# A chunked linear-attention stage in front of a dense layer: chunks of 64 steps of two batches on 64x64 tiles of the matrix array

## The chip, the cores and the metric

The kernel runs on one core of a Trainium2 chip. The core has a matrix engine (TensorE: PE for its matmuls, PEld for its weight loads), a vector engine (DVE), a scalar engine (ACT), GpSimd (POOL) and SyncE (SP), which here only issues DMAs. TensorE reads SBUF and writes the eight PSUM banks; DVE and ACT read PSUM, POOL does not. The metric is the device time of one launch in microseconds (us); lower is better.

## The reference

Four batches, eight heads, 768 steps, head size 48. For each batch and head, with a decay w and a bonus u per channel:

```python
for t in range(S):
    y[t] = r[t] @ (state + outer(u * k[t], v[t]))
    state = w[:, None] * state + outer(k[t], v[t])
```

The outputs are laid side by side over the heads (3072 tokens by 384), and a dense block follows: `h = x @ w_in` (384 by 2048), `g = h - tanh(h)`, `out = g @ w_out` (2048 by 384). The weights arrive as 64-bit floats, so the kernel rebuilds 32-bit ones from their bits.

## The kernel before

**Units and blocks.** The attention is cut into 24 units of one batch and one chunk of 128 steps (`C`). Two units make a block of 256 tokens, held transposed in a tile `xt`, and the dense layer runs block by block. `drive` (L177) sets the order: blocks 0 and 1 of the attention are woven with the 28 steps that load and convert the weights; then `dense(j)` is woven with the attention of block j+2, for j from 0 to 9; `dense(10)` and `dense(11)` have no attention beside them. The framework orders each engine's instructions by priority and by its own estimate of readiness and puts the semaphores in; an engine then works through its list in order.

**One unit** (`unit`, L310) has six steps, between which the weave may put dense work. The heads lie in four pairs, each padded to two times 64 rows or columns.

- POOL scales k and r by powers of the decay (`kw` L317, `rw` L318), PE transposes both (four 128x128 transposes each, L323), ACT copies them to SBUF as `kT` and `rT` (L325). POOL multiplies r, k and u (L330, L331).
- DVE sums that product to the bonus `du` (L334), POOL forms `dv` = v times `du` (L336), PE forms the scores `lev` = k against r, eight matmuls on 48 rows, which lie in the upper or the lower half of the array (L342).
- DVE copies the strictly earlier half of the scores to `at` by a mask (two instructions, L345).
- PE forms `y_p`: four matmuls with the running state (L350, not in a batch's first chunk) and eight with `at` and v (L354); DVE adds `dv` (L357).
- PE forms the state's increment `kv_p` (L362, not in a batch's last chunk), DVE adds it to the state (two instructions, L369), POOL multiplies by the chunk's decay (L373). PE transposes y (three transposes, L376) and ACT copies it to `xt` (L377).

**Dense** (`make_dense`, L118): for each pair of 128-column slices of `w_in`, six matmuls of 256 columns give `h` (L129); ACT, DVE and POOL form `g` in ten instructions (L140 to L149), of which DVE has five; two pairs later, four matmuls of 384 columns add to `o` (L155). ACT copies `o` out (L169), SP stores it (L171).

**Records.** All data are 32-bit floats, and the profile shows every matmul that is not a transpose as two weight loads and two matmuls: eight matmuls of `lev` are x16 in a row.

**Queues and tables.** r, k and v are loaded two units ahead by three DMAs on SP's queue (`fetch`, L300). Weights come by one DMA per tile on ACT's queue (L90) into two staging tiles, and are converted by one ACT, five DVE and two POOL instructions (L97 to L104). Ahead of all units, DVE makes the tables of the powers of the decay (L252 to L259), which PE turns (L265). A second version of the attention (`anywhere`, L384) runs only when a decay lies outside W_LOW to W_HIGH; with these inputs it does not.

Of the kernel before, what the change touches and what calls it, by code (L numbers as in the profile page):

```python
# [27 lines left out]
W_LOW, W_HIGH = 0.7, 1.4  # L28

C = 128  # L30
PAD = 64
AHEAD = 2
L = 2
# [13 lines left out]
class Dims:  # L47
    def __init__(self, r, moe_w_in):
        self.B, self.H, self.S, self.D = r.shape
        self.DM, self.DFF = moe_w_in.shape  # L50
        self.NP = self.H // 2
        self.NCH = self.S // C
        self.NU = self.NCH * self.B
        self.NK = self.DM // 128
        self.NF = self.DFF // 128
# [19 lines left out]

def weight_steps(nc, stage, w_in_sb, w_out_sb, moe_w_in, moe_w_out, d):
    V, A, G = nc.vector, nc.scalar, nc.gpsimd
    w_in_v = moe_w_in.rearrange("(ko ki) f -> ki ko f", ki=128)
    w_out_v = moe_w_out.rearrange("(ko ki) f -> ki ko f", ki=128)

    def weight(dst, src, cols):
        if src.dtype == F32:
            return lambda: nc.scalar.dma_start(out=dst, in_=src)


        assert src.dtype == I64
# [22 lines left out]
    for q in range(d.DFF // 512):  # L109
        for ko in range(d.NK):  # L110
            sl = slice(q * 512, (q + 1) * 512)
            weights.append(weight(w_in_sb[:, ko, sl], w_in_v[:, ko, sl], 512))
        for f in range(4 * q, 4 * q + 4):
            weights.append(weight(w_out_sb[:, f, :], w_out_v[:, f, :], d.DM))
# [3 lines left out]
def make_dense(nc, work, gpool, ps_d, w_in_sb, w_out_sb, m1b, m2b, out, d):  # L118
# [3 lines left out]
    def dense(j, xt):  # L122
# [43 lines left out]
        for i in range(L):  # L166
            c, b = divmod(L * j + i, d.B)
# [36 lines left out]
def near(ctx, tc, r, k, v, w, u, out, shared, weights):  # L204
# [42 lines left out]
    by = fixed("by", [128, NP, C + 1])  # L247
    plus = fixed("plus", [128, NP, C + 1])
    power = fixed("power", [128, NP, C + 1])
    inverse = fixed("inverse", [128, NP, C + 1])  # L250
    V.memset(by[:, :, 0:1], 0.0)
    V.tensor_copy(by[:, :, 1:], wcol[:, :, None].to_broadcast([128, NP, C]))  # L252
# [5 lines left out]
    wn = fixed("wn", [128, NP])  # L258
    V.tensor_copy(wn[:, :, None], power[:, :, C : C + 1])  # L259

    def turned(name, src, at):

        ps = ps_a.tile([128, 512], F32, name="tab_p", tag="tp")
        for p in range(NP):
            T.transpose(ps[:, p * 128 : (p + 1) * 128], src[:, p, at : at + C], ident)  # L265
        t = fixed(name, [128, H, D])
        A.copy(t, ps.rearrange("s (h d) -> s h d", h=H)[:, :, :D])
        return t

    w_up = turned("w_up", power, 0)  # L270
    w_down = turned("w_down", inverse, 1)

# [6 lines left out]
    before = fixed("before", [128, C])  # L279
    G.memset(before, 1.0)  # L280
    G.affine_select(out=before, in_=before, compare_op=ALU.is_ge, fill=0.0, base=-1,
                    pattern=[[1, C]], channel_multiplier=-1)
    before = before.bitcast(I32)

    def zeroed(name, count, shape):
        tiles = [fixed(f"{name}{i}", shape) for i in range(count)]
        for t in tiles:
            G.memset(t, 0.0)
        return tiles

    kws = zeroed("kw", 2, [128, H, PAD])
    rws = zeroed("rw", 2, [128, H, PAD])
    ats = [zeroed(f"at{i}_", 2, [128, NP, C]) for i in range(2)]
    states = zeroed("state", B, [128, NP, 2, D])

    dense = make_dense(nc, work, gpool, ps_d, shared["w_in"], shared["w_out"], shared["m1b"],
                       shared["m2b"], out, d)
    loaded = {}

    def fetch(n):  # L300
        c, b = divmod(n, B)
        rows = slice(c * C, (c + 1) * C)
        tiles = []
        for name, src in (("kt", k), ("rt", r), ("vt", v)):
            t = load.tile([128, H, D], F32, name=name, tag=name)
            nc.sync.dma_start(out=t, in_=src[b, :, rows, :].rearrange("h t d -> t h d"))
            tiles.append(t)
        loaded[n] = tiles

    def unit(n, xt, slot):  # L310

        c, b = divmod(n, B)
# [3 lines left out]
        state, kw, rw = states[b], kws[n % 2], rws[n % 2]  # L316
        G.tensor_tensor(kw[:, :, :D], kt, w_down, ALU.mult)  # L317
        G.tensor_tensor(rw[:, :, :D], rt, w_up, ALU.mult)  # L318
        turned = []
        for name, src in (("kT", kw), ("rT", rw)):  # L320
            ps = ps_a.tile([128, NP, C], F32, name="t_p", tag="tp")
            for p in range(NP):
                T.transpose(ps[:, p, :], src[:, 2 * p : 2 * p + 2, :].rearrange("t h d -> t (h d)"), ident)  # L323
            t = work.tile([128, NP, C], F32, name=name, tag=name)
            A.copy(t, ps)  # L325
            turned.append(t)
        kT, rT = turned

        rk = work.tile([128, H, D], F32, name="rk", tag="rk")
        G.tensor_tensor(rk, rt, kt, ALU.mult)  # L330
# [4 lines left out]
        dv = work.tile([128, H, D], F32, name="dv", tag="dv")  # L335
        G.tensor_tensor(dv, vt, du[:, :, None].to_broadcast([128, H, D]), ALU.mult)  # L336

        at = [ats[i][n % 2] for i in range(2)]
        lev = [ps_a.tile([128, NP, C], F32, name=f"lev{i}", tag=f"lev{i}") for i in range(2)]
        for p in range(NP):  # L340
            for i in range(2):
                T.matmul(lev[i][:, p], kT[HEAD[i], p, :], rT[HEAD[i], p, :], start=True, stop=True)  # L342
        yield
        for i in range(2):
            V.copy_predicated(at[i], before[:, None].to_broadcast([128, NP, C]), lev[i])  # L345
        yield
        y_p = ps_a.tile([128, NP, 2, D], F32, name="y_p", tag="ky")
        for p in range(NP):
            if c:
                T.matmul(y_p[:, p].rearrange("t i e -> t (i e)"), rT[:, p, :],  # L350
                         state[:, p].rearrange("d i e -> d (i e)"),
                         start=True, stop=False, skip_group_check=True)
            for i in range(2):
                T.matmul(y_p[:, p, i, :], at[i][:, p, :], vt[:, 2 * p + i, :],  # L354
                         start=c == 0, stop=True, skip_group_check=True)
        y = work.tile([128, H * D], F32, name="y", tag="y")
        V.tensor_tensor(y, y_p.rearrange("t p i e -> t (p i e)"), dv.rearrange("t h e -> t (h e)"), ALU.add)  # L357
        yield
        if c < d.NCH - 1:
            kv_p = ps_a.tile([128, NP, 2, D], F32, name="kv_p", tag="ky")  # L360
            for p in range(NP):
                T.matmul(kv_p[:, p].rearrange("d i e -> d (i e)"),  # L362
                         kw[:, 2 * p : 2 * p + 2, :].rearrange("s h d -> s (h d)"),
                         vt[:, 2 * p : 2 * p + 2, :].rearrange("s h e -> s (h e)"),
                         start=True, stop=True)
            for i in range(2):
                rows = HEAD[i]
                if c:
# [283 lines left out]
```

## Time and profile before

| | |
|---|---|
| median of 3 runs (lowest, highest) | 768.67 us (766.57, 769.08) |
| the profiled execution, its own time | 770.07 us |
| its span, first to last instruction | 768.3 us |
| mean granted TensorE clock | 0.961 of full speed |
| busy share of the span: PE, DVE, POOL, ACT | 88%, 69%, 49%, 38% |
| matmuls and weight loads recorded | 3280 and 3280 |

The span is cut into the time before about 200 us, in which the weights are converted, and the time after it. A matmul's recorded duration holds its way through the array, so that neighbours overlap; what one costs in a stream is the distance between starts. The chain of waits is followed back from the last instruction to what released each step.

### The profile page before, as it was taken

To read this page: it belongs to the slowest core of one execution; us is meant where nothing else is said; L and a number is where in the kernel's file an instruction comes from. 1 tells how busy PE (TensorE), PEld (TensorE's weight loads), DVE (VectorE), ACT (ScalarE), POOL (GpSimd) and SP (SyncE) were. 2 spreads that over 40 slices of the span, in tenths; PEclk is the share of its full clock that TensorE was granted. 3 is DMA by queue.
4 is the path that set the end of the run, shared out by engine and by line. 5 is a ranking of instruction groups with operands and counts; after the bars stand their busy time and mean duration, and the time that the engine had idled before them with its cause. 6 is when DMAs were issued, how large, how long until landed. Compare 5 with 4: busy or idle time off the path is not lost.

```text
span 768.3 us, 9268 instructions
## 1 busy us (share of the span) xinstructions
PE 678.2 (88%) x3280; PEld 513.8 (67%) x3280; DVE 532.9 (69%) x779; ACT 289.7 (38%) x511; POOL 379.9 (49%) x312
## 2 busy tenths in 40 slices
PE   1357769376999999999999999999999999999996
PEld 0246547254776876876776777778778777777774
DVE  9779999989675664864765765666646646566573
ACT  1114232214343533533534434334435345344432
POOL 6979966767344544534634543543534323223221
PEclk9999778767899999999999999999999999999999
DMA  7333343232011101102111111111100000000000
GB/s 185 87 105 106 93 113 83 80 79 68 22 31 37 37 12 47 25 11 52 22 27 36 32 22 31 32 21 32 22 20 21 1 22 0 1 21 0 22 1 26
DMA packets 82986, 32.35 MB, mean 42 GB/s; under 512 B 76146, under 2 KB 79347, under 8 KB 82931
## 3 DMA queue, kind: packets, MB, share of 16 engines
q1 hardware_dynamic: 78898, 19.08, 11.2%
q10 hardware_dynamic: 4032, 12.58, 5.4%
q8 instruction: 28, 0.46, 0.2%
q14 instruction: 28, 0.22, 0.1%
HBM read 26.94 MB, written 4.72 MB: 41 GB/s over the span
## 4 chain that ended last, share of the span: by engine, by line
PE 74%; DVE 12%; POOL 7%; issue 3%; DMA 2%; ACT 1%; ACTq 0%; DVEq 0%; POOLq 0%
PE h L129 31%; PE o L155 28%; PE y_p L354 5%; PE lev L342 3%; PE y_p L350 3%; PE t_p L323 2%; POOL part L103 2%; PE kv_p L362 2%; DVE cube L148 2%; DMA st<-in_moe_w_in_dram 2%; DVE cube L147 1%; DVE part L98 1%; DVE st L100 1%; DVE g L149 1%; POOL rk L330 1%
## 5 line engine op out<-in xcount | busy, mean ns | idle before, releaser
L129 PE MATMUL h<-xt,w_in_sb 128*128 128x256 f32 x1152 | 280.2, 390 | 11.9 <-POOL w_in_sb L104 11.6
L155 PE MATMUL o<-w_out_sb,g 128*128 128x384 f32 x768 | 272.4, 501 | 17.8 <-DVE g L149 17.8
L144 POOL TENSOR_SCALAR small<-s 128x512 f32<-128x512 f32 x96 | 147.9, 1541 | 213.7 <-ACT s L140 204.7
L129 PEld LDWEIGHTS h<-xt,w_in_sb 128*128 128x128 f32 x1152 | 215.9, 195 | 45.4 <-POOL w_in_sb L104 12.3
L155 PEld LDWEIGHTS o<-w_out_sb,g 128*128 128x128 f32 x768 | 147.9, 195 | 108.7 <-DVE g L149 12.9
L145 DVE SCALAR_TENSOR_TENSOR cube<-s,h 128x512 f32<-128x512 f32 x96 | 65.8, 685 | 176.6 <-ACT th L141 176.4
L140 ACT ACTIVATE s<-h 128x512 f32<-128x512 f32 x96 | 57.3, 597 | 191.7 <-issue 131.6
L149 DVE COPY_PREDICATED g<-small,cube 128x512 f32<-128x512 int32 x96 | 85.6, 892 | 5.2
L148 DVE SCALAR_TENSOR_TENSOR cube<-q,cube 128x512 f32<-128x512 f32 x96 | 80.0, 834 | 8.2
L147 DVE SCALAR_TENSOR_TENSOR cube<-q,cube 128x512 f32<-128x512 f32 x96 | 74.8, 779 | 0.0
L354 PE MATMUL y_p<-vt,at 128*128 128x48 f32 x384 | 58.9, 282 | 12.9 <-DVE at L345 12.9
L142 ACT ACTIVATE q<-s,m1b 128x512 f32<-128x512 f32 x96 | 69.3, 722 | 0.0
L143 ACT ACTIVATE q<-s,m2b 128x512 f32<-128x512 f32 x96 | 69.0, 718 | 0.6 <-DVE cube L148 0.6
L354 PEld LDWEIGHTS y_p<-vt,at 128*128 128x128 f32 x384 | 55.5, 208 | 17.7 <-DVE at L345 15.3
L146 DVE TENSOR_TENSOR g<-h,th 128x512 f32<-128x512 f32 x96 | 65.5, 682 | 0.0
L141 ACT ACTIVATE th<-h 128x512 f32<-128x512 f32 x96 | 56.8, 591 | 0.0
L336 POOL TENSOR_TENSOR dv<-vt,du 128x384 f32<-128x384 f32 x24 | 24.2, 1007 | 60.5 <-DVE y L357 60.5
L103 POOL TENSOR_TENSOR part<-part,st 128x384 f32<-128x384 f32 (+1 forms) x28 | 35.8, 1279 | 26.0 <-issue 14.1
L318 POOL TENSOR_TENSOR rw<-rt,w_up 128x384 f32<-128x384 f32 x24 | 29.2, 1217 | 38.2 <-PE t_p L323 37.4
L377 ACT COPY xt<-x_p 128x384 f32<-128x384 f32 x24 | 11.5, 480 | 83.7 <-PE x_p L376 83.7
L342 PEld LDWEIGHTS lev<-rT,kT 48*128 48x128 f32 x384 | 27.3, 212 | 23.1 <-ACT rT L325 13.8
L342 PE MATMUL lev<-rT,kT 48*128 48x128 f32 x384 | 32.5, 313 | 11.3 <-ACT rT L325 11.3
(75 smaller groups left out, 596.8 us busy)
## 6 DMA issues: line engine op xcount, KB each, us to landing
st<-in_moe_w_in_dram ACTq DMA_DIRECT2D x12, 512.0 KB, 3.9
st<-in_moe_w_out_dram ACTq DMA_DIRECT2D x16, 384.0 KB, 3.1
kt<-in_k_dram SPq DMA_DIRECT2D x24, 192.0 KB, 2.8
rt<-in_r_dram SPq DMA_DIRECT2D x24, 192.0 KB, 2.6
vt<-in_v_dram SPq DMA_DIRECT2D x24, 192.0 KB, 2.6
out_dram<-o SPq DMA_DIRECT2D x24, 192.0 KB, 1.9
ub<-in_u_dram SPq DMA_DIRECT2D x1, 192.0 KB, 5.2
wcol<-in_w_dram SPq DMA_DIRECT2D x2, 0.8 KB, 4.6
```

What stands on the lines that cost most here:

```text
L129: T.matmul(h[:, z], w_in_sb[:, kk, (f + z) * 128 : (f + z + 1) * 128], xt[:, kk].rearrange("p b t -> p (b t)"), start=kk == 0, stop=kk == ...
L142: A.activation(q1, s, AF.Square, bias=m1b)
L143: A.activation(q2, s, AF.Square, bias=m2b)
L144: G.tensor_scalar(small, s, SMALL, None, ALU.is_lt)
L145: V.scalar_tensor_tensor(cube, s, C4, hf, ALU.mult, ALU.mult)
L146: V.tensor_tensor(gf, hf, th, ALU.subtract)
L147: V.scalar_tensor_tensor(cube, q1, K1, cube, ALU.add, ALU.mult)
L148: V.scalar_tensor_tensor(cube, q2, K2, cube, ALU.add, ALU.mult)
L149: V.copy_predicated(gf, small.bitcast(I32), cube)
L155: T.matmul(outs[i], g[:, z, i * C : (i + 1) * C], w_out_sb[:, f + z, :], start=f + z == 0, stop=f + z == d.NF - 1)
L342: T.matmul(lev[i][:, p], kT[HEAD[i], p, :], rT[HEAD[i], p, :], start=True, stop=True)
L354: T.matmul(y_p[:, p, i, :], at[i][:, p, :], vt[:, 2 * p + i, :], start=c == 0, stop=True, skip_group_check=True)
```

## The change

A unit becomes one chunk of 64 steps (`SHORT`) of two batches, the two batches in the upper and lower 64 partitions; there are still 24 units, now 12 chunks by two pairs of batches. The matmuls of the unit (`lev`, the state's part of y, the part of `at` and v, and `kv`) are cut so that each uses at most 64 rows and 64 columns of the array, and the loops go over the four 64x64 quarters in turn; `put` keeps them in program order. y is formed transposed, so that it needs no transposes; `dv` goes, since `du` now stands on the diagonal of `at`. r is transposed unscaled and scaled by DVE on the way out of PSUM. The heads 6 and 7 of y are moved by six small DMAs to the rows 48 to 63 and 112 to 127 of `xt`, and the rows of `w_in` are loaded in the order that fits (four DMAs per tile in place of one). Loads and stores are split by batch: six loads per unit, two stores per output tile. The unit has five steps in place of six. `anywhere` gets the same row order.

```diff
@@ weight_steps
+def row_blocks(d):
+    for i in range(2):
+        yield i * PAD, None, i * d.D, d.D
+        for kk in range(d.NK):
+            yield i * PAD + d.D, kk, (2 * d.NK + i) * d.D + kk * d.NX, d.NX
...
-            nc.scalar.dma_start(out=st, in_=src)
+            for to, src in pieces:
+                nc.scalar.dma_start(out=st[to], in_=src)
@@ make_dense
-            row = b * d.S + c * C
-            nc.sync.dma_start(out=out[row : row + C, :], in_=o)
+            runs = rows(L * j + i)
+            n = C // len(runs)
+            for z, row in enumerate(runs):
+                nc.sync.dma_start(out=out[row : row + n, :], in_=o[z * n : (z + 1) * n])
@@ near, tables
-    by = fixed("by", [128, NP, C + 1])
+    by = fixed("by", [128, NP, SHORT + 1])
...
-    w_up = turned("w_up", power, 0)
-    w_down = turned("w_down", inverse, 1)
+    w_up, twice = (fixed(x, [128, NP, 2, SHORT]) for x in ("w_up", "twice"))
+    V.tensor_copy(w_up, power[:, :, None, :SHORT].to_broadcast([128, NP, 2, SHORT]))
+    V.tensor_copy(twice, inverse[:, :, None, 1:].to_broadcast([128, NP, 2, SHORT]))
+    w_all = power[:, None, :, SHORT:].to_broadcast([128, 2, NP, D])
+    ps = ps_a.tile([128, 2, 512], F32, name="x_ps", tag="x_ps")
...
+    same = fixed("same", [128, SHORT])
+    V.tensor_tensor(same, ident[:, :SHORT], ident[:, SHORT:], ALU.add)
...
+    yk_ps = ps_a.tile([128, 2, 512], F32, name="yk_ps", tag="yk_ps")
+    turned = ps[:, :, 256:]
+    lev = ps[:, :, :256].rearrange("s i (p t) -> s i p t", p=NP)
+    y_ps = yk_ps[:, :, :256].rearrange("e z (p t) -> e z p t", p=NP)
+    kv_ps = yk_ps[:, :, 256 : 256 + NP * D].rearrange("d z (p e) -> d z p e", p=NP)
@@ fetch
+        for t, src in ((rt, r), (kt, k), (vt, v)):
+            for z in range(2):
+                nc.sync.dma_start(out=t[HALF[z], :, :D], in_=src[half * 2 + z, :, rows, :].rearrange("h t d -> t h d"))
@@ unit
         G.tensor_tensor(kw[:, :, :D], kt, w_down, ALU.mult)
-        G.tensor_tensor(rw[:, :, :D], rt, w_up, ALU.mult)
...
+        for src in (rt, kw):
             for p in range(NP):
...
+            if src is rt:
+                V.tensor_tensor(halves(rT), turned, halves(w_up), ALU.mult)
+            else:
+                A.copy(halves(kT), turned)
...
-        G.tensor_tensor(dv, vt, du[:, :, None].to_broadcast([128, H, D]), ALU.mult)
+        G.tensor_tensor(at, same[:, None, None, :].to_broadcast([128, 2, NP, SHORT]),
+                        du.rearrange("s (p i) -> s i p", i=2)[:, :, :, None].to_broadcast([128, 2, NP, SHORT]),
+                        ALU.mult)
+        for p in range(NP if ch else 0):
+            for z in range(2):
+                for i in range(2):
+                    put(y_ps[i * PAD : (i + 1) * PAD, z, p], state[HEAD[i], z, p], rT[HEAD[i], p, z],
+                        start=p == 0, stop=False)
+        for p in range(NP):
+            for z in range(2):
+                for i in range(2):
+                    put(lev[HALF[z], i, p], kT[HEAD[i], p, z], rT[HEAD[i], p, z], start=True, stop=True)
+        yield
+        V.copy_predicated(at, before, lev)
+        yield
         for p in range(NP):
             for i in range(2):
+                for z in range(2):
+                    put(y_ps[i * PAD : (i + 1) * PAD, z, p], vt[HALF[z], 2 * p + i], at[HALF[z], i, p],
+                        start=p == 0 and not ch, stop=p == NP - 1)
+        last = ch == d.S // SHORT - 1
+        if not last:
+            for p in range(NP):
+                for i in range(2):
+                    for z in range(2):
+                        put(kv_ps[i * PAD : (i + 1) * PAD, z, p], kw[HALF[z], 2 * p + i], vt[HALF[z], 2 * p + i, :D],
+                            start=True, stop=True)
+        A.copy(xt[:, :, slot].rearrange("e p (z t) -> e z p t", z=2), y_ps[:, :, :NK])
+        rest = work.tile([128, 2, SHORT], F32, name="rest", tag="rest")
+        A.copy(rest, y_ps[:, :, NK])
         for i in range(2):
+            for kk in range(NK):
+                nc.sync.dma_start(out=xt[i * PAD + D : (i + 1) * PAD, kk, slot],
+                                  in_=rest[i * PAD + kk * d.NX :][: d.NX].rearrange("x z t -> x (z t)"))
+        yield
+        if not last:
+            now = state[:, :, :, :D]
+            if ch:
+                V.tensor_tensor(now, kv_ps, now, ALU.add)
+            else:
+                V.tensor_copy(now, kv_ps)
+            G.tensor_tensor(now, now, w_all, ALU.mult)
+        yield
-    drive(d, work, unit, dense, fetch, weights, 6)
+    drive(d, work, unit, dense, fetch, weights, 5)
```

## Rows read from the trace of the kernel before

**Rows 1.** The page, part 1: busy time, share of the span and instructions.
```profile
PE 678.2 (88%) x3280; PEld 513.8 (67%) x3280; DVE 532.9 (69%) x779; ACT 289.7 (38%) x511; POOL 379.9 (49%) x312
```
**Rows 2.** Windows: busy time of PE, PEld, DVE, ACT, POOL; clock; DMA.
```profile
200.00:680.00 480.00, 474.63 (x2431) 363.35 (x2430) 302.24 (x449) 201.37 (x356) 202.70 (x158) 1.00 0.11 25
0.00:200.00 200.00, 121.68 (x539) 91.69 (x540) 177.86 (x250) 49.58 (x87) 152.63 (x138) 0.85 0.38 96
```
**Rows 3.** Chain of waits in order of time: start, us, what.
```profile
354.49 2.85 PE o L155 x8
...
409.16 2.85 PE o L155 x8
...
712.50 7.74 PE o L155 x24
...
754.22 7.75 PE o L155 x24
```
**Rows 4.** Timeline of PE: start, us, line, xcount, idle before and its releaser.
```profile
409.16 2.85 PE L155 MATMUL o<-w_out_sb,g 128*128 128x384 f32 x8 [0.90 <-DVE g L149]
411.84 0.60 PE L323 MATMUL t_p<-ident,kw 128*128 128x128 f32 x4
412.28 1.03 PE L129 MATMUL h<-xt,w_in_sb 128*128 128x256 f32 x4
413.14 0.63 PE L323 MATMUL t_p<-ident,rw 128*128 128x128 f32 x4
413.61 1.89 PE L129 MATMUL h<-xt,w_in_sb 128*128 128x256 f32 x8
415.43 1.16 PE L342 MATMUL lev<-rT,kT 48*128 48x128 f32 x16
416.52 5.45 PE L129 MATMUL h<-xt,w_in_sb 128*128 128x256 f32 x24
421.81 2.74 PE L155 MATMUL o<-w_out_sb,g 128*128 128x384 f32 x8
424.39 0.36 PE L350 MATMUL y_p<-state,rT 128*128 128x96 f32 x2
...
427.00 1.53 PE L129 MATMUL h<-xt,w_in_sb 128*128 128x256 f32 x6
428.36 1.03 PE L362 MATMUL kv_p<-vt,kw 128*128 128x96 f32 x8
429.23 0.49 PE L376 MATMUL x_p<-ident,y 128*128 128x128 f32 x3
429.55 1.46 PE L129 MATMUL h<-xt,w_in_sb 128*128 128x256 f32 x6
```
**Rows 5.** Groups by line and shape: busy, mean ns; idle before, releaser.
```profile
L345 DVE COPY_PREDICATED at<-before,lev 128x512 f32<-128x512 int32 x48 | 33.7, 725 | 1.0 <-PE lev L342 1.0
L357 DVE TENSOR_TENSOR y<-y_p,dv 128x384 f32<-128x384 f32 x24 | 13.3, 555 | 9.3 <-PE y_p L354 9.2
L146 DVE TENSOR_TENSOR g<-h,th 128x512 f32<-128x512 f32 x96 | 65.5, 682 | 0.0
L325 ACT COPY rT<-t_p 128x512 f32<-128x512 f32 x24 | 14.0, 585 | 27.7 <-PE t_p L323 18.8 <-POOL part L103 8.9
L318 POOL TENSOR_TENSOR rw<-rt,w_up 128x384 f32<-128x384 f32 x24 | 29.2, 1217 | 38.2 <-PE t_p L323 37.4 <-POOL part L103 0.8
L336 POOL TENSOR_TENSOR dv<-vt,du 128x384 f32<-128x384 f32 x24 | 24.2, 1007 | 60.5 <-DVE y L357 60.5
L103 POOL TENSOR_TENSOR part<-part,st 128x512 f32<-128x512 f32 x12 | 17.4, 1450 | 18.6 <-issue 11.0 <-ACT st L97 7.2 <-DVE part L102 0.4
L257 DVE RECIPROCAL inverse<-power 128x516 f32<-128x516 f32 x1 | 3.4, 3365 | 0.0
```
**Rows 6.** Timeline of the first 60 us: two issues of a DMA.
```profile
14.32 0.34 ACTq L90 DMA_DIRECT2D st<-in_moe_w_in_dram  x1
...
33.17 0.37 SPq L306 DMA_DIRECT2D rt<-in_r_dram  x1
```

More of the change, by code (lines that the diff above doesn't have):

```diff
@@ L283, in near, with padded @@
     before = before.bitcast(I32)
-    def zeroed(name, count, shape):
-        tiles = [fixed(f"{name}{i}", shape) for i in range(count)]
+    before = before[:, None, None, :].to_broadcast([128, 2, NP, SHORT])
+    def padded(name, count):
+        tiles = [fixed(f"{name}{i}", [128, H, PAD]) for i in range(count)]
         for t in tiles:
-            G.memset(t, 0.0)
+            G.memset(t[:, :, D:], 0.0)
         return tiles
-    kws = zeroed("kw", 2, [128, H, PAD])
-    rws = zeroed("rw", 2, [128, H, PAD])
@@ L303, in fetch @@
[L303 to L308, printed above, removed]
+        ch, half = divmod(n, 2)
+        rows = slice(ch * SHORT, (ch + 1) * SHORT)
+        kt = load.tile([128, H, D], F32, name="kt", tag="kt")
+        rt, vt = rts[n % (AHEAD + 1)], vts[n % (AHEAD + 1)]
@@ L310, in unit, with halves, put @@
+        for t, src in ((rt, r), (kt, k), (vt, v)):
+            for z in range(2):
+                nc.sync.dma_start(out=t[HALF[z], :, :D], in_=src[half * 2 + z, :, rows, :].rearrange("h t d -> t h d"))
+        loaded[n] = kt, rt, vt
+    def halves(t):
+        return t.rearrange("d (y p) z t -> d y (p z t)", y=2)
+    def put(*args, **how):
+        tc.keep_in_program_order(T.matmul(*args, skip_group_check=True, **how))
     def unit(n, xt, slot):
-        c, b = divmod(n, B)
+        ch, half = divmod(n, 2)
@@ L334, in unit @@
         V.tensor_reduce(du, rk, axis=mybir.AxisListType.X, op=ALU.add)
[L335 to L339 removed]
+        at = work.tile([128, 2, NP, SHORT], F32, name="at", tag="at")
+        G.tensor_tensor(at, same[:, None, None, :].to_broadcast([128, 2, NP, SHORT]),
+                        du.rearrange("s (p i) -> s i p", i=2)[:, :, :, None].to_broadcast([128, 2, NP, SHORT]),
+                        ALU.mult)
@@ L356, in unit @@
[L356 to L368, printed above, removed]
-                    V.tensor_tensor(state[rows, :, i, :], kv_p[rows, :, i, :], state[rows, :, i, :], ALU.add)
-                else:
-                    V.tensor_copy(state[rows, :, i, :], kv_p[rows, :, i, :])
-            both = state.rearrange("d p i e -> d p (i e)")
-            G.tensor_tensor(both, both, wn[:, :, None].to_broadcast([128, NP, 2 * D]), ALU.mult)
@@ L551, in unit @@
                          start=c == 0, stop=True, skip_group_check=True)
-        y = work.tile([128, H * D], F32, name="y", tag="y")
-        V.tensor_tensor(y, y_p.rearrange("t p i e -> t (p i e)"), dv.rearrange("t h e -> t (h e)"), ALU.add)
+        y = work.tile([128, NK, 2, PAD], F32, name="y", tag="y")
+        V.tensor_tensor(y[:, :, :, :D], y_p[:, :NK], dv[:, : 2 * NK].rearrange("t (p i) e -> t p i e", i=2), ALU.add)
+        for i in range(2):
+            V.tensor_tensor(y[:, :, i, D:], y_p[:, NK, i].rearrange("t (k x) -> t k x", k=NK),
+                            dv[:, 2 * NK + i].rearrange("t (k x) -> t k x", k=NK), ALU.add)
         yield
```

107 lines of the change are left out of this document (46 added, 61 removed).

## The prediction

> **What bounds the kernel now.** I read the page first: PE is busy 88% of the span, no other engine above 69% [rows 1]. A share is a mean over stages, so the windows come next. From 200 to 680 us PE works 474.6 of 480 us at full granted clock, DVE 302; before 200 us it is the other way round, DVE 177.9 of 200 and PE 121.7 at a clock of 0.85 [rows 2]. So there are two stages: the front, which DVE sets while the weights are converted, and the steady one, which PE sets. In the chain of waits the steady stage is a period: the same eight `o` matmuls start at 354.49 and 409.16, so a block with two units takes 54.67 us. Blocks without attention end 754.22 - 712.50 = 41.72 us apart [rows 3]. Attention costs 12.95 us per block, all of it PE's.
>
> The timeline splits that by distances between starts [rows 4]. Four `h` from 412.28 to 413.14 take 0.215 each (256 columns), eight `o` from 421.81 to 424.39 0.3225 each (384): 128 columns more are 0.107 us, and next to nothing is fixed. One unit costs:
> - transposes: 412.28 - 411.84 = 0.44 and 413.61 - 413.14 = 0.47, together 0.91;
> - `lev`: the eight `h` before it would end at 413.61 + 8 x 0.215 = 415.33; it starts at 415.43 and the next `h` at 416.52, and these 24 need 5.29 in place of 5.16: 1.32 us;
> - `y_p`: 427.00 - 424.39 = 2.61, and the six `h` behind it spend 1.36 for 1.29: 2.68. That is 24 matmuls at 0.112; the moving side has only 48 or 96 columns, so the weight load of 128 columns sets the pace;
> - `kv_p` 0.87 (429.23 - 428.36) and the transposes of y 0.32: 1.19.
>
> The sum is 6.10 per unit. Twice that and the 0.90 us wait of each block [rows 4] make 13.1, against 12.95.
>
> `lev` is the row to learn from. Its 16 matmuls are 128 columns wide; one by one they would need 16 x 0.112 = 1.79, yet the whole detour costs 1.32. The two 64-row halves of the array therefore work at once: 8 x 0.112 = 0.90, and 0.43 is left for going into the half-array form and back.
>
> **The change on PE.** A unit now has 64 matmuls of 64 columns with 64 weight columns, which is 128 records for the 48 before. If both sides halve as the columns do, a step of a tile lasts 0.112 / 2 = 0.056. The state's part of y uses two quarters (rows and columns of the same half): 32 records, two at once, 16 steps. `lev`, `at` with v, and `kv` go over all four quarters: 32 records each, 8 steps each, if four run at once. That is 40 steps or 2.24 us. The four kinds lie in two groups (step 2: state and `lev`; step 4: the other two), so there are two detours of 0.43. The eight transposes stay (0.91), those of y go. Sum 0.91 + 2.24 + 0.86 = 4.01, against 6.10.
>
> Blocks 0 to 2, six units, belong to the front: `dense(0)` ends near 200 us. The steady units are 6 to 23. Units 6 to 19 gain 2.09 each: 29.3. Units 20 and 21 had no `kv` before and now have it (the last chunk is units 22 and 23 alone): 4.01 - 5.23 = -1.22 each, 2.4 together. Units 22 and 23: 3.56 - 5.23 = -1.67 each, 3.3. Together -35.0 us.
>
> **New waits of PE.** ACT copied both transposes; now `rT` comes from DVE (nearest row `g` L146, 0.68, against ACT's 0.585 [rows 5]), and the transposes of `kw` need the same PSUM, so they stand behind that product, with all of PE behind them. DVE works 63% of this stage, so the product can queue behind a dense instruction. Also `at` must now be multiplied by `du` on POOL before the mask copy, where `dv` was needed only at the end; three steps of the weave lie between. Dense work can fill both, as it fills the way from `kw` to `rw` now. The one standing wait in the trace is 0.90 per block [rows 4]. I take 0.3 per unit, 5.4 us over 18 units; the ends are -0.45 (the standing wait goes too, -8 us) and 0.9 (16 us).
>
> **The other engines.** DVE per unit: two mask copies (1.45) become one as wide as either (0.73), the addition of y (0.56) goes, the product with `rT` (0.68) comes, the two short state additions become one: about -0.6. POOL: `rw` (1.22) and `dv` (1.01) go, `at`, 512 wide as L103 is (1.45), comes: -0.8 [rows 5]. ACT swaps two copies for one and a small one. In the steady stage all this lies beside PE. In the front six units give DVE -3.6, and the table's reciprocal, half as long, -1.7; the other table instructions, some shorter, three new, I put at nothing.
>
> **DMAs.** Each w_in tile takes four issues on ACT's queue in place of one, 0.34 each [rows 6]: 36 more, 12 us of an engine that works 50 of the front's 200 [rows 2], but each tile lands up to 1.0 us later. Exposed are between 0 and 12 us; as two staging tiles hide most, I take 4. Front: -5.3 + 4 = about -1, ends -7 and +10. SP issues six loads, six moves of `rest` and two stores per unit, 14 x 0.37 = 5.2 us [rows 6] of some 25. The moves wait for ACT's copy, with the next loads and stores behind them; the loads run two units ahead, and `xt` is read a whole block after it is filled, so nobody waits. Without that lead each unit would show a landing of a few us. `anywhere` does not run.
>
> **Sum.** -35.0 + 5.4 - 1 = -30.6 on the profiled execution's 770.07 gives 739.5; that execution stands 1.4 above the median of 768.67, so 738.
>
> **Rivals.**
> *Two at a time.* The trace shows the upper and lower half at work together, never two column halves. If the column halves of one row half take turns, four kinds need 64 steps: 3.58 us, a unit 5.35. Units 6 to 19 gain 0.75, 20 and 21 lose 0.12, 22 and 23 gain 0.78: -11.9, with the other terms -7.5, 761. For it: no row with more than two. Against it: nothing shows the two directions to differ. The Trainium skill (TensorE: Matmul & The Clock Gate, Part 1) says that starts never come closer than about 25 ns however few the columns. This speaks against four at once, which wants one per 14 ns; by it the sum would come to an estimated 755. The rows here show no starts that dense.
>
> *Slower: small matmuls do not get cheaper.* The place is the pace of the two groups on PE. If a record of 64 columns takes as long as one of 128 (a load or an issue that does not shrink), the 64 steps last 0.112: 7.2 us. A unit costs 8.9, units 6 to 19 lose 2.8, 20 and 21 3.7, 22 and 23 1.9: +50, with the other terms +54, 823. It decides from (6.10 - 0.91 - 0.86) / 128 = 0.034 us per record: above that the change loses. `lev`, the densest row, has 0.056 on the mean. Against it: `h` and `o` show time in proportion to columns down to no visible rest. For it: no weight load under 128 columns stands in the trace. The Trainium skill (TensorEngine Tiling (Array Packing), Performance Considerations) warns of this: each matmul has some 60 cycles of overhead, so one column lasts as long as sixty, and a dimension that is already small should not be cut. At 64 columns its limit is just not reached.
>
> *Waits eat it.* If the product on DVE or the chain over `at` holds PE 1.9 us per unit, 35 us are gone: no change, 769. Only 0.90 per block is seen now.
>
> **How the numbers follow.** Forecast 0.47, two at a time 0.20, waits 0.08, slower 0.25. Differences below 0.3% are taken as none. So faster 0.67, same 0.08, slower 0.25. The forecast's own range is 719 (-35 - 8 - 7) to 760 (-35 + 16 + 10). The whole range must reach past 761 and into the slower case, since only a fifth may be left out: some two fifths of that case lie at prices from 0.034, which gives 773, to 0.041, which adds 0.007 x 128 records x 18 units = 16 and gives about 790. The corner below 722, where all ends are good at once, I leave out: 722 to 790.
>
> **What would show it.** Right: the steady period falls to about 51 us; the group of the state's part and `lev` takes about 1.8 us with its detour, the other 1.3; PE's idle time stays near 1 to 1.5 us per block; the front ends near 200 us. Two at a time: both groups near 2.2. Slower: both near 4 and a period of about 60. Waits: `t_p` or `y_p` preceded by idle time ended by DVE or POOL. Wrong altogether: if the groups are broken up by dense matmuls, each break costs another 0.43.

## The result, and the profile after

The changed kernel takes 725.73 us (median of 4 runs, 724.9 to 726.02) against 768.5 for the kernel before (4 runs, 766.57 to 769.08): ratio 0.9446 [0.9427, 0.9464]. Forecast were 738 us (722 to 790). The profiled execution took 725.77 us with a span of 724.0.

In the profile after, the conversion of the weights stands in L113 to L120 (L97 to L104 before); `o` is L177, its copy L190, `h` L151, the last instruction of `g` L171. All small matmuls go through one helper and show as L348; they are told apart by their tiles. The transposes are L363, DVE's product that makes `rT` L365.

One row per kernel splits the time: the copies of `o`, with the start of the first and of the last. Before, then after (a copy of 128x384 by ACT, 24 times: shortest, median and longest in ns, first and last start in us):

```profile
L169 ACT COPY o<-o x24: 479/479/480, 200.1 to 762.0; 128x384 f32<-128x384 f32 x24
```

```profile
L190 ACT COPY o<-o x24: 479/479/480, 188.0 to 717.0; 128x384 f32<-128x384 f32 x24
```

The first start is where the front ends. It moved from 200.1 to 188.0: **-12.1**. From there to the last copy it is 561.9 before and 529.0 after: **-32.9**. This split is used for all runs below, as "front" and "rest"; it is read from the one profiled execution of a run, which lies within 1.6 us of the run's median, except where it is said. The forecast had -1 for the front and -29.6 for the rest (-35.0 on PE, +5.4 of waits).

Next the windows (busy us and instructions of PE, PEld, DVE, ACT, POOL; granted clock; DMA share; GB/s), which answer to [rows 2]:

```profile
0.00:200.00 200.00, 106.86 (x1100) 78.28 (x1101) 158.77 (x249) 52.03 (x97) 137.89 (x129) 0.81 0.44 98
200.00:640.00 440.00, 437.02 (x3672) 320.09 (x3671) 283.31 (x416) 192.12 (x352) 192.12 (x147) 1.00 0.15 30
```

The stages are what they were: behind 200 us PE works 437.0 of 440 us, at full granted clock. In the first 200 us DVE works 158.8 where it worked 177.9. The chain gives the new period, as [rows 3] gave the old one:

```profile
395.43 2.85 PE o L177 x8
...
445.74 2.85 PE o L177 x8
...
667.56 7.74 PE o L177 x24
...
709.27 7.75 PE o L177 x24
```

A block with two units now takes 445.74 - 395.43 = 50.31 us (54.67 before), one without any still 709.27 - 667.56 = 41.71. Attention costs 8.60 per block in place of 12.95. PE's timeline shows one unit and the end of the one ahead of it (start, duration, engine, line, tiles, shapes, count):

```profile
439.68 5.45 PE L151 MATMUL h<-xt,w_in_sb 128*128 128x256 f32 x24
445.74 2.85 PE L177 MATMUL o<-w_out_sb,g 128*128 128x384 f32 x8 [0.61 <-DVE g L171]
448.52 0.69 PE L348 MATMUL yk_ps<-at,vt 64*64 64x64 f32 x32
...
460.04 0.60 PE L363 MATMUL x_ps<-ident,rt 128*128 128x128 f32 x4
460.48 1.89 PE L151 MATMUL h<-xt,w_in_sb 128*128 128x256 f32 x8
462.26 0.63 PE L363 MATMUL x_ps<-ident,kw 128*128 128x128 f32 x4
462.72 1.03 PE L151 MATMUL h<-xt,w_in_sb 128*128 128x256 f32 x4
463.59 2.74 PE L177 MATMUL o<-w_out_sb,g 128*128 128x384 f32 x8
466.26 1.08 PE L348 MATMUL yk_ps<-rT,state 48*64 48x64 f32 x29
...
467.24 0.64 PE L348 MATMUL x_ps<-rT,kT 48*64 48x64 f32 x30
467.81 2.86 PE L151 MATMUL h<-xt,w_in_sb 128*128 128x256 f32 x12
470.50 2.74 PE L177 MATMUL o<-w_out_sb,g 128*128 128x384 f32 x8
...
475.67 2.74 PE L177 MATMUL o<-w_out_sb,g 128*128 128x384 f32 x8
478.35 0.69 PE L348 MATMUL yk_ps<-at,vt 64*64 64x64 f32 x32
478.86 0.63 PE L348 MATMUL yk_ps<-vt,kw 64*64 64x48 f32 x32
479.42 5.43 PE L177 MATMUL o<-w_out_sb,g 128*128 128x384 f32 x16
```

By distances between starts: transposes 0.44 + 0.46; the state's part with `lev` 467.81 - 466.26 = 1.55; `at` with v and `kv` 479.42 - 478.35 = 1.07. The twelve `h` behind the first group take 2.69 where 12 x 0.215 = 2.58 would do, so each group leaves 0.11 to what follows it. It also costs something ahead of it: the eight `o` before each group take 2.67 and 2.68 (466.26 - 463.59, 478.35 - 475.67) where 8 x 0.3225 = 2.58 would do, 0.09 and 0.10 more. With both, the groups cost 1.75 and 1.28 us, where 1.8 and 1.3 had been named. One unit is 0.90 + 1.75 + 1.28 = 3.93 us, against 6.10 before and 4.01 forecast; twice that and the wait below make 8.47 of the 8.60. The first row shows the wait that is left, 0.61, where [rows 4] had 0.90; from 200 to 640 us it comes up six times, 2.9 us in all.

### The profile page after: what moved, and what is told of

Read it like the earlier page. It is cut to its first block, busy times and chain, and to the rows that moved or that the text cites. A ratio compares the mean times of both kernels' runs of the same rounds, so it can differ in the third digit from the quotient of the medians.

```text
span 724.0 us, 13305 instructions
## 1 busy us (share of the span) xinstructions
PE 620.9 (86%) x5060; PEld 453.2 (63%) x5060; DVE 492.4 (68%) x739; ACT 279.5 (39%) x510; POOL 352.6 (49%) x289
## 4 chain that ended last, share of the span: by engine, by line
PE 68%; DVE 12%; DMA 8%; POOL 6%; issue 4%; SPq 1%; ACT 0%; ACTq 0%; DVEq 0%; POOLq 0%
PE o L177 33%; PE h L151 27%; PE yk_ps L348 4%; DMA st<-in_moe_w_out_dram 4%; DMA rt<-in_r_dram 3%; POOL part L119 3%; PE x_ps L363 2%; POOL rk L370 2%; POOL rk L371 2%; DVE st L116 1%; DVE part L114 1%; DVE w_in_sb L117 1%; DVE part L118 1%; DVE w_in_sb L115 1%; DVE cube L170 1%
## 5 line engine op out<-in xcount | busy, mean ns | idle before, releaser
L151 PE MATMUL h<-xt,w_in_sb 128*128 128x256 f32 x1152 | 276.4, 389 | 20.6 <-POOL w_in_sb L120 20.5
L177 PE MATMUL o<-w_out_sb,g 128*128 128x384 f32 x768 | 270.0, 498 | 11.8 <-DVE g L171 11.8
L151 PEld LDWEIGHTS h<-xt,w_in_sb 128*128 128x128 f32 x1152 | 217.1, 194 | 59.8 <-POOL w_in_sb L120 22.9
L177 PEld LDWEIGHTS o<-w_out_sb,g 128*128 128x128 f32 x768 | 146.8, 194 | 102.4 <-issue 11.6
L171 DVE COPY_PREDICATED g<-small,cube 128x512 f32<-128x512 int32 x96 | 78.5, 818 | 5.6
L348 PE MATMUL yk_ps<-rT,state 48*64 48x64 f32 x704 | 27.7, 234 | 24.3 <-DVE state L416 19.3
L113 ACT ACTIVATE st<-st 128x384 f32<-128x384 uint32 (+1 forms) x28 | 17.1, 610 | 73.3 <-POOL part L119 34.5
L348 PEld LDWEIGHTS yk_ps<-rT,state 48*64 48x64 f32 x704 | 24.6, 146 | 33.1 <-issue 28.2
L376 POOL TENSOR_TENSOR at<-same,du 128x512 f32<-128x512 f32 x24 | 30.9, 1286 | 23.9 <-PE yk_ps L348 21.4
L365 DVE TENSOR_TENSOR rT<-x_ps,w_up 128x512 f32<-128x512 f32 x24 | 16.4, 685 | 29.3 <-PE x_ps L363 29.3
L374 DVE TENSOR_REDUCE du<-rk 128x8 f32<-128x384 f32 x24 | 13.2, 550 | 33.3 <-POOL rk L371 33.3
L370 POOL TENSOR_TENSOR rk<-rt,kt 128x384 f32<-128x384 f32 x24 | 26.6, 1109 | 16.5 <-DMA rt<-in_r_dram 9.5
```

Source lines behind the costliest of these rows:

```text
L151: T.matmul(h[:, z], w_in_sb[:, kk, (f + z) * 128 : (f + z + 1) * 128], xt[:, kk].rearrange("p b t -> p (b t)"), start=kk == 0, stop=kk == ...
L171: V.copy_predicated(gf, small.bitcast(I32), cube)
L177: T.matmul(outs[i], g[:, z, i * C : (i + 1) * C], w_out_sb[:, f + z, :], start=f + z == 0, stop=f + z == d.NF - 1)
L348: tc.keep_in_program_order(T.matmul(*args, skip_group_check=True, **how))
```

## The experiments

The changed kernel is the base of every run unless another is named; each ratio is to the kernel before, which ran beside it (median 768.9 to 769.6). The first two runs ask what a step costs and whether the quarters work together, the others what made the front shorter.

**Two quarters at a time.** The loops of `lev`, `at` with v and `kv` go first over one column half, then over the other:

```diff
-        for p in range(NP):
-            for z in range(2):
+        for z in range(2):
+            for p in range(NP):
...
-            for p in range(NP):
-                for i in range(2):
+            for i in range(2):
+                for p in range(NP):
```

> The changed kernel with the loops of three kinds of matmul turned round (the scores, the part of at with v, kv), so that all matmuls of one column half come first and those of the other after them; every instruction stays, only their order differs. Theory, four quarters work at once: now only two do, each of the three kinds needs 16 steps of 0.058 us in place of 8, 24 x 0.058 = 1.4 us more per unit, 25 us over 18 steady units: 751 us, and the group of at with v and kv grows from 1.1 to 2.0 us. Rival, the column halves of one row half take turns anyway and the gain is that of smaller matmuls: no change, 726 us.

734.22 us (733.67 to 735.68), ratio 0.9561 [0.9526, 0.9597]; front 187.9, rest 537.8, so 8.8 more in the rest and none in the front. The order counts, but for a third of what was expected, and neither expectation was met. PE's timeline of this run shows why:

```profile
471.00 1.08 PE L348 MATMUL yk_ps<-rT,state 48*64 48x64 f32 x29
...
472.84 2.86 PE L151 MATMUL h<-xt,w_in_sb 128*128 128x256 f32 x12
...
483.38 0.80 PE L348 MATMUL yk_ps<-at,vt 64*64 64x64 f32 x26
483.97 0.26 PE L348 MATMUL yk_ps<-vt,kw 64*64 64x48 f32 x2
484.01 0.23 PE L348 MATMUL yk_ps<-at,vt 64*64 64x64 f32 x2
484.06 0.22 PE L348 MATMUL yk_ps<-vt,kw 64*64 64x48 f32 x2
484.07 0.23 PE L348 MATMUL yk_ps<-at,vt 64*64 64x64 f32 x2
...
484.85 5.43 PE L177 MATMUL o<-w_out_sb,g 128*128 128x384 f32 x16
```

The groups last 1.84 (472.84 - 471.00) and 1.47 us, 0.69 more per unit. Fully in turn they would need 24 steps more, 24 x 0.056 = 1.34. The rows in between show what saves the other half: matmuls of `kv`, which begin on the idle column half, start while those of `at` with v still go on in the other. Six records of `kv` start so, three steps or 0.17 us. The program changes column halves at four such places per unit (once within `lev`, once within `at` with v, between that and `kv`, once within `kv`), and four times 0.17 is what was saved; the rows tell only the one place apart, so for the other three this is inferred. 18 x 0.69 = 12.4, less 2.2 for waits that this longer period covers (2.9 to 0.7 us from 200 to 640), is 10.2, and about 9.1 with the 0.27 that each wait costs beyond what it shows (last section; four fewer), against 8.8 measured.

**More groups.** Two more yields in each unit, so that dense work may come between the state's part and `lev`, and between `at` with v and `kv`:

```diff
+        yield
         for p in range(NP):
             for z in range(2):
                 for i in range(2):
                     put(lev[HALF[z], i, p], ...
...
+        yield
         if not last:
...
```

> The changed kernel with two more steps in the weave, between the state's part and the scores and between at with v and kv, so that dense matmuls may come between: 64 stretches of quarter-array matmuls in the program in place of 46, the same instructions. Theory, each way into the quarter form and back costs about 0.43 us of PE: 18 more cost 7.7 us, some of it in the front: 730 to 734 us. Rival, the way in and out overlaps with the dense stream and was no real cost: 726 us.

731.07 us (729.04 to 732.3), ratio 0.9513 [0.9484, 0.9541]; front 189.9, rest 532.8 (+3.8). The total lies where the theory put it, and its price nearly holds. In the rest only one unit per block came apart, and then the timeline has each kind by itself:

```profile
467.12 1.15 PE L348 MATMUL yk_ps<-rT,state 48*64 48x64 f32 x32
468.19 1.13 PE L151 MATMUL h<-xt,w_in_sb 128*128 128x256 f32 x4
...
471.84 0.69 PE L348 MATMUL x_ps<-rT,kT 48*64 48x64 f32 x32
472.46 2.86 PE L151 MATMUL h<-xt,w_in_sb 128*128 128x256 f32 x12
...
477.83 0.69 PE L348 MATMUL yk_ps<-at,vt 64*64 64x64 f32 x32
478.45 2.86 PE L151 MATMUL h<-xt,w_in_sb 128*128 128x256 f32 x12
```

`lev` alone, 8 steps, takes 0.62; `at` with v alone 0.62; two such kinds together, 16 steps, 1.07 (after). So 8 steps cost 1.07 - 0.62 = 0.45: **0.056 a step**, as forecast. The state's part alone, 32 records on two quarters, takes 1.07 too: 16 steps, as forecast. What is left is 0.62 - 0.45 = 0.17 for going in and out, with the 0.10 ahead of a group and the 0.11 behind it: a detour costs **0.38**, where 0.43 was taken. In the rest there are 53 such groups in place of 36: 17 x 0.38 = 6.5, less 1.7 for the waits that are covered (2.9 to 1.2 us) and 0.8 for what these three waits cost beyond what they show, is 4.0, against 3.8 measured.

**The front: r on POOL again.** r is scaled on POOL ahead of its transposes and copied by ACT, as before the change; the rest of the change stays. POOL then needs its turned table again (four transposes and a copy at the start) and two more padded tiles:

```diff
...
+        rw = rws[n % 2]
+        G.tensor_tensor(rw[:, :, :D], rt[:, :, :D], w_upt, ALU.mult)
...
-        for src in (rt, kw):
+        for src in (rw, kw):
...
-                V.tensor_tensor(halves(rT), turned, halves(w_up), ALU.mult)
+                A.copy(halves(rT), turned)
```

> The changed kernel with one part undone: r is scaled on POOL ahead of the transposes again (1.2 us more of POOL per unit) and ACT copies the result out of PSUM (0.68 us less of DVE per unit). Theory, in the front DVE's instructions are stretched while POOL works, so POOL's time is what the front pays for: the front gets 3 to 8 us longer, 729 to 734 us, and DVE's conversion instructions before 190 us get longer on the mean. Rival, the front is set by DVE's own instructions: 6 x 0.68 = 4 us less, 722 us.

730.36 us (729.55 to 732.47), ratio 0.9508 [0.948, 0.9536]. Front 198.9 (+10.9), rest 523.8 (-5.2). Two effects of opposite sign lie in one number. The front loses most of what the change had gained there. DVE's conversion instructions, though, did not get longer as expected: they take 99.6 us in the first 200, against 98.9 in the changed kernel. The rest gains, because DVE no longer makes `g` late: from 200 to 640 us PE is busy for all 440 us.

**The same part alone, in the kernel before.** r goes unscaled to its transposes, in a padded tile, and DVE scales it on the way out of PSUM. With it go POOL's table `w_up` (four transposes and a copy at the start) and the clearing of two whole tiles, for which the padding of three is cleared; nothing else of the change:

```diff
...
-        G.tensor_tensor(rw[:, :, :D], rt, w_up, ALU.mult)
...
-            A.copy(t, ps)
+            if src is rt:
+                V.tensor_tensor(t, ps, power[:, :, :C], ALU.mult)
+            else:
+                A.copy(t, ps)
...
```

> The kernel before with one part of the change alone: r is transposed unscaled and scaled by DVE on the way out of PSUM, so that POOL has 1.2 us less per unit and DVE 0.68 more. Theory (POOL sets the front as much as DVE): the front ends 6 to 11 earlier, the steady stage loses up to 5 as POOL's turn gained 5 there: 760 to 768. Rival (DVE alone sets the front): 9 products of 0.68 in the front make it 6 longer, 770 to 780.

758.86 us (758.1 to 759.27), ratio 0.9861 [0.9837, 0.9885]: 10.7 us less, a quarter of the whole gain. Front 191.2 (-8.9), rest 559.8 (-2.1). DVE got more instructions, and the front that it was said to set became shorter. The groups of the conversion on DVE in the first 200 us show how, before and then in this run (busy us, mean ns, idle ahead):

```profile
L100 DVE TENSOR_SCALAR st<-st 128x384 uint32<-128x384 uint32 (+1 forms) x28 | 19.8, 708 | 0.5
...
L101 DVE SCALAR_TENSOR_TENSOR w_out_sb<-st,w_out_sb 128x384 f32<-128x384 uint32 x16 | 13.6, 851 | 0.1
```

```profile
L100 DVE TENSOR_SCALAR st<-st 128x384 uint32<-128x384 uint32 (+1 forms) x28 | 14.5, 519 | 0.5
...
L101 DVE SCALAR_TENSOR_TENSOR w_out_sb<-st,w_out_sb 128x384 f32<-128x384 uint32 x16 | 11.8, 737 | 0.1
```

The same instructions are shorter here, where POOL does less beside them. Over all eight groups of the conversion (L98 to L102) it is 112.8 us before, 98.3 here and 98.9 in the changed kernel. This sum is not what the front follows in general: with r on POOL again it was 99.6 and the front 10.9 later, and with one DMA per tile (below) it is 109.3 and the front 3.4 earlier. In the rest, PE has no wait on record from 200 to 640 us here, though DVE forms the product; so the product as such does not make `g` late. That the order on DVE's queue does is likely, but not shown.

**Idle work on POOL, then on DVE.** Two multiplications that nobody reads are added to each of units 0 to 5, once on POOL, once on DVE:

```diff
+        if n < 6:
+            for x in range(2):
+                idle = work.tile([128, H, D], F32, name="idle", tag="idle")
+                G.tensor_tensor(idle, rt[:, :, :D], ub, ALU.mult)
```

> Two multiplications of 128x384 that nobody reads are added on POOL in each of units 0 to 5: 12 x 1.2 = 14 us of POOL in the front. Theory (POOL and DVE set the front together, and POOL's own length counts): front 9 to 14 later, 735 to 740. Rival (DVE alone sets it, as the prediction had it): POOL's work counts only as far as DVE is stretched beside it; DVE's instructions of the front stand some 45 us above the fastest of their form beside 138 us of POOL, a third, so 14 us of POOL give 4 to 5: 730.

> The same two multiplications of 128x384 on DVE in place of POOL in units 0 to 5: 12 x 0.55 = 6.6 us of DVE, more where POOL runs beside it. Rival (DVE alone sets the front): 6.6 to 9 later, 732 to 735. Theory (DVE idles 39 of the front's 200 us waiting for POOL and weights): most of it falls into that idle time, 726 to 730.

On POOL 733.61 us (732.63 to 737.56), ratio 0.9532 [0.9507, 0.9558], front 197.8 (+9.8); on DVE 728.63 (726.98 to 729.69), ratio 0.9466 [0.9439, 0.9493], front 191.9 (+3.9). The added instructions, on POOL and on DVE:

```profile
L375 POOL TENSOR_TENSOR idle<-rt,ub x12: 994/1063/1444, 9.1 to 75.4; 128x384 f32<-128x384 f32 x12
```

```profile
L375 DVE TENSOR_TENSOR idle<-rt,ub x12: 534/1291/1634, 8.7 to 67.2; 128x384 f32<-128x384 f32 x12
```

The profiled execution of the first is 3.9 us above its median, so totals are safer than fronts. By totals, POOL's 12 x 1.06 = 13 us cost 7.9 and DVE's 12 instructions, 13.5 us in all, 2.9. POOL's price lies between the two expectations; DVE alone, which would have given 730 and 732 to 735, is off in both. On DVE the median is 1291 ns where the shortest is 534: beside POOL they more than double.

**Tiles cleared whole.** POOL clears the kw, rt, vt and state tiles whole at the start, in place of their padding:

```diff
-            G.memset(t[:, :, D:], 0.0)
+            G.memset(t, 0.0)
```

> The kw, rt, vt and state tiles are cleared whole on POOL at the start, as before, in place of their 16 padding columns per head: 10 tiles at about 0.42 in place of 0.23, so POOL clears for some 2 us longer. In the kernel before one DVE instruction of 0.4 us took 4.4 beside these memsets. Theory (this start is part of the 12 us that the front gained): front 2 to 4 later, 728 to 730. Rival (the first weights land later than either anyway): 725 to 727.

729.01 us (726.85 to 731.57), ratio 0.9478 [0.9454, 0.9502], front 192.2 (+4.2). The number is the theory's, the cause is not shown: the loads into rt now come behind its memsets, which they don't in the kernel before (rt is first issued at 8.8 us, in the changed kernel at 2.5), and the first product of r and k on POOL starts at 18.6 us in place of 10.9. Inconclusive.

**One DMA per tile of w_in.**

```diff
+            pieces = [(slice(0, 128), moe_w_in[ko * 128 : (ko + 1) * 128, sl])]
```

> The changed kernel with each w_in tile loaded by one DMA in place of four; the rows of w_in stay in the order in which they lie in memory, so the order that fits the moved heads is left out. The prediction took 4 us (0 to 12) for the four issues. Theory (a cost that the front hides behind DVE and POOL): 0 to 1 less, 725 to 726. Rival (each tile lands 1 us later and DVE stands for it): 4 less, about 722.

719.06 us (717.69 to 719.75), ratio 0.9343 [0.9319, 0.9366]: 6.7 less than the changed kernel, and less than either expectation. Front 184.6 (-3.4), rest 525.4 (-3.6, of which the first block behind the front has most). So the four pieces are not hidden. ACT's largest wait in the first 200 us of the changed kernel stands ahead of its part of the conversion, where the issues of the pieces stand on its queue too (engine, line, what for; us, times, longest):

```profile
ACT st L113 <- POOL part L119: 34.5, 6, 7.8
```

Here this wait comes to 23.6 us. But the one for `w_in` to land grows from 10.0 to 27.4, and all waits ahead of L113 add up to 72.0 us here and 73.3 in the changed kernel. So the trace does not show whether the issues themselves, the later landing or the order cost the 6.7 us.

**Four staging tiles in place of two.**

```diff
-    with tc.tile_pool(name="stage", bufs=2) as stage:
+    with tc.tile_pool(name="stage", bufs=4) as stage:
```

> The changed kernel with four staging tiles for the weights in place of two. Theory, the front is now set by the landing of the weights into two staging tiles (about 26 us of DMA stand in the chain of waits before 205 us): the front gets 10 to 20 us shorter, 706 to 716 us. Rival, the front is set by the conversion on DVE and POOL: 722 to 726 us.

740.19 us (738.22 to 741.75), ratio 0.9625 [0.9589, 0.9662], front 199.6: slower, against every theory. The last conversion on POOL starts at 159.2 us, 27 earlier than in the changed kernel (186.0), and still the front ends 11.6 later. PE's timeline shows what stood in its place:

```profile
115.26 1.83 PE L348 MATMUL yk_ps<-rT,state 48*64 48x64 f32 x29 [19.45 <-DVE state L416]
...
150.62 1.83 PE L348 MATMUL yk_ps<-rT,state 48*64 48x64 f32 x29 [23.83 <-DVE state L416]
```

The addition to the state stands on DVE's queue behind conversions that can now run ahead (from 99.2 to 114.6 us DVE does nothing else); the attention of the front's last units comes late by that. Weights and attention share DVE, and here what one gained the other lost.

**A version with both gains.** r is scaled by DVE in units 0 to 5 (where POOL is short of time) and by POOL from unit 6 on (where DVE's lateness costs):

```diff
...
+        early = n < 6
+        rw = rt if early else rws[n % 2]
+        if not early:
+            G.tensor_tensor(rw[:, :, :D], rt[:, :, :D], w_upt, ALU.mult)
...
```

> r is scaled on POOL and copied by ACT from unit 6 on, and by DVE (as in the changed kernel) in units 0 to 5. With POOL in all units the steady stage (first to last block with attention) took 481.4 us against 486.7 and PE had no wait left in it, but the front ended 10.9 later. Theory (the steady stage's waits come from DVE's product, the front's loss from POOL): front as in the changed kernel, steady stage 5.3 shorter, 720 to 721, faster than both kernels. Rival (the 5.3 came from the later front, which left more work done ahead): 725 to 726.

726.23 us (725.6 to 727.13), ratio 0.9442 [0.942, 0.9464]: front 194.2 (+6.2), rest 523.8 (-5.2). The rest is as expected. The front is not, though its units work as in the changed kernel; only POOL's table and two padded tiles were added at the start. The run with r on POOL throughout has the same start and differs from this one in units 0 to 5 alone: its front ends at 198.9, so 6.2 of its 10.9 us come with the start, and r itself makes 198.9 - 194.2 = 4.7. On DVE's queue a sum stands ahead of conversions and waits for POOL:

```profile
23.52 0.55 DVE L386 TENSOR_REDUCE du<-rk 128x8 f32<-128x384 f32 x1 [6.00 <-POOL rk L383]
```

In the changed kernel that sum of unit 1 waits 0.90. So the table was moved to unit 6:

> As the run in which POOL scales r from unit 6 on, but the turned table that POOL then needs (four transposes and a copy) and the clearing of two tiles are moved from the start into unit 6. That run had the shorter steady stage (439.5 against 445.0 us over nine blocks) but a front 6.2 us longer, in which DVE stood 6 us behind one sum of unit 1 at 17 to 23 us. Theory (the front's loss came from the extra work at the start, which turned the order of the first instructions): front as in the changed kernel, 720 to 721, faster than both. Rival (any change of the program shifts the order of the front by some microseconds): 722 to 727.

723.78 us (722.52 to 725.0), ratio 0.9408 [0.9384, 0.9433]: front 190.8 (+2.8), rest 524.0 (-5.0). About 2 us better than the change itself, though the intervals of the two ratios overlap. The rival had its part: the front moved by 2.8 though nothing in it was meant to change.

Last, two of the four pieces of each w_in tile were issued by SP:

```diff
-                nc.scalar.dma_start(out=st[to], in_=src)
+                (nc.sync if to.stop - to.start == d.NX else nc.scalar).dma_start(out=st[to], in_=src)
```

> As the run with the table in unit 6, but of the four pieces of each w_in tile the two of 16 rows (64 KB) are issued by SP in place of ACT. With one piece per tile the changed kernel was 6.7 us faster, 36 issues fewer on ACT. Theory (the cost is the issues on ACT, which stand in front of ACT's own work): half of them leave ACT, 3 to 4 us less than the 723.8 of the run it starts from: 720. Rival (SP waits there for a free staging tile with the loads of the next units queued behind it): nothing gained, or 2 to 8 us slower: 724 to 732.

734.13 us (734.04 to 734.67), ratio 0.9543 [0.9521, 0.9564], front 204.8, 14 later than in the run it starts from. SP's queue of the first 200 us:

```profile
SPq L106 <- POOL part L119: 58.6, 10, 12.4
SPq L341 <- DMA st<-in_moe_w_out_dram: 21.8, 6, 5.3
```

SP stands 58.6 us for a free staging tile, and the loads of r, k and v (L341) are queued behind it. The rival holds.

## Why the prediction was right, and where it was off

**PE's gain.** The likeliest case came true: four quarters work at once, and half the columns take half the time, 0.056 us a step, 40 steps. 32 matmuls of `at` with v start within 0.51 us (478.35 to 478.86). By the floor of some 25 ns between starts that the Trainium skill gives (TensorE: Matmul & The Clock Gate, Part 1) they would need an estimated 0.8; the trace disagrees, and the 755 us worked out from that floor didn't come. The detour of 0.43 was a little too dear: 0.38. The unit of 4.01 measured 3.93, and the two groups came out at 1.75 and 1.28 us where "about 1.8" and "1.3" had been named, so here the mechanism was right and not only the number. The slower rival and "two at a time" fell; turning the loops so that column halves take turns gives back 8.5 us.

**New waits.** Forecast at +5.4 us, they are not there: the standing wait is 0.61 where it was 0.90. Neither the product that makes `rT` nor `at` has a wait of PE on record in the rest; all waits there are for `g`. The product isn't free all the same: with r on POOL the rest is 5 us shorter, in three runs. By these terms the rest should have lost more than 35 us, and it lost 32.9. Counted from one block's last copy of `o` to the next one's, five steady blocks gain 4.4 to 5.0 us each, but the first behind the front only 1.6 (47.3 to 45.7). Perhaps the kernel before had more of that block's work done when its front ended; the runs don't show it.

**The front is the step that failed.** "Front: -5.3 + 4 = about -1, ends -7 and +10" measured -12.1, beyond its end. Between the profiled executions the gain is 44.3 us where 30.6 was forecast, and 11.1 of the 13.7 us lie here; the rest, with -32.9 for -29.6, has 3.3. The total stayed inside the stated range by luck: the range had been kept wide for other terms, and this one left its own. The DMA term was of the right kind: 4 us taken, 6.7 found, 3.4 of it in the front (what of the four pieces costs it is not shown). The relief was undersized: without the splitting the front would have gained 12.1 + 3.4 = 15.5. The error is the sentence "the front, which DVE sets", from which POOL's relief was put at nothing. The runs show that POOL's length counts beside DVE's: POOL work added there costs 0.6 us per us (7.9 for 13), the same work on DVE 0.2 (2.9 for 13.5). Taking r from POOL, with the table that goes with it, gives 8.9 although DVE gets 0.68 more per unit; r in units 0 to 5 alone, with the same table, makes 4.7.

Part of the coupling is plain in the trace. Every DVE conversion instruction of the changed kernel that takes over 1.3 times the shortest of its form has a POOL instruction beside it; the longest of L117 took 1596 ns, the shortest 542. But two DVE instructions of the units never stretch, after:

```profile
L365 DVE TENSOR_TENSOR rT<-x_ps,w_up x24: 669/684/693, 17.0 to 610.6; 128x512 f32<-128x512 f32 x24
...
L374 DVE TENSOR_REDUCE du<-rk x24: 539/552/555, 13.6 to 544.7; 128x8 f32<-128x384 f32 x24
...
L116 DVE TENSOR_SCALAR st<-st x28: 341/416/1215, 14.1 to 182.1; 128x384 uint32<-128x384 uint32 x16, 128x512 uint32<-128x512 uint32 x12
...
L117 DVE SCALAR_TENSOR_TENSOR w_out_sb<-st,w_out_sb x16: 542/548/1596, 34.8 to 183.0; 128x384 f32<-128x384 uint32 x16
```

The first two read one operand from SBUF (the product's other comes from PSUM), L117 reads two; L116 reads one and stretches as well. This is what the Trainium skill says (SBUF — State Buffer, Who interferes with whom): DVE with two SBUF inputs and a GpSimd instruction that reads SBUF shut each other out for a whole instruction; DVE with one doesn't contend, unless it runs in a two-port mode, which the Trainium skill gives to tensor_scalar (L116) and not to tensor_tensor. The trace agrees, with 1596 and 1215 ns for L117 and L116 and at most 693 for L365. So moving r's scaling to DVE took from POOL a multiplication that could block DVE, and gave DVE one that did not stretch. The prediction counted instructions and left this out. How much of the front this makes is not shown: with r back on POOL, DVE's conversion took 99.6 us, 0.7 more than in the changed kernel and 5.7 more than in the run with the same start (93.9).

**Left open.** Of the 15.5 us some 9 are r's scaling with its table, if the parts add up, and 4.7 to 8.9 the scaling itself. The others (`dv`, the memsets, the halved tables, PE's own gain, one unit's share of which lies in the front) weren't taken apart: single edits that should not touch the front moved it by 2.8 to 6.2 us through the order on the queues, so parts of that size, the 4.7 among them, can't be told from it. That POOL's length counts rests on the idle work above all; what the start contributes is open. A unit with all its small matmuls in one group was not tried.

## What to carry to other kernels

Small matmuls on 64x64 quarters paid here with loops that go round all four quarters: the price was that of the longest quarter, plus some 0.4 us for each stretch between full-size matmuls. Where two engines feed one stage, count the work taken from each of them, and look which DVE instructions stretch beside POOL; here those with two SBUF operands and TENSOR_SCALAR did, the product with one operand in PSUM did not. An edit that is good in one stage may be bad in another, as r on POOL was: split the time by stage for every run, and choose by unit.

## What the runs showed of the hardware

- Matmuls of different column halves interleave: in the run with turns, `kv` began while `at` with v still went on, and half of the turn-taking (0.65 of 1.34 us per unit) was saved.
- In the kernel before, one DVE instruction on a single row of 384 elements took 4.40 us beside POOL's memsets; the same instruction took 0.47 in the changed kernel. It took 0.64 in the run that clears whole tiles, also beside memsets, so what held it for 4.4 us is not shown:

```profile
L237 DVE TENSOR_SCALAR okr<-okr x1: 4404/4404/4404, 2.7 to 2.7; 1x384 f32<-1x384 f32 x1
```

```profile
L261 DVE TENSOR_SCALAR okr<-okr x1: 469/469/469, 3.1 to 3.1; 1x384 f32<-1x384 f32 x1
```

- A wait of 0.61 us cost PE 0.88. From the 24 `h` ahead of it to the group behind the eight `o` the changed kernel needs 448.52 - 439.68 = 8.84 us. The same stretch without a wait, in the run with the table in unit 6, needs 497.23 - 489.27 = 7.96:

```profile
489.27 5.45 PE L151 MATMUL h<-xt,w_in_sb 128*128 128x256 f32 x24
...
497.23 0.69 PE L350 MATMUL yk_ps<-at,vt 64*64 64x64 f32 x32
```
